# The first weight load of a two-branch decode kernel, cut after 16 partitions

## The chip, the cores and the metric

The kernel runs on one core of a Trainium2 chip. The metric is the time of one execution on the device in microseconds; the median of three runs of the kernel before is 825.76 us (825.72 to 825.88).

## What is computed

Two attention layers, A and B, each decode one token and their outputs are joined. Both have 32 heads of 128, a key and a value cache of 16384 positions, and bf16 data.

```
q   = x @ wq                                   # x: 512, wq: 512 x 4096
p   = softmax(q . k * 128**-0.5)               # per head
o   = p @ v
out = o @ wo                                   # wo: 4096 x 512
A: all 16384 positions;  B: the last 4096 positions alone
result = concat(A's out, B's out)              # 1024 numbers
```

Nearly all of the work is to read the caches: 134 MB of keys and as much of values for A, a quarter of that for B, and 4 MiB for each of the four weight matrices.

## The kernel before

The order of the work is written out by hand (`manual_schedule`), so each engine and each queue runs its instructions in the order of the program. The work goes through 20 steps `T`. A step of A takes two heads, a step of B eight; B's are steps 0, 7, 13 and 19. A step loads an 8 MiB tile of keys (for B in two halves of four heads) and later an equal tile of values. Keys stand in a ring of two buffers (`kring`), values in one buffer (`vring`).

For each half of a key tile VectorE multiplies the keys by q (line 227) and adds up along the head dimension in a tree (lines 233 and 237). TensorE and ScalarE do the softmax of the step before and its product with the values (`pv`, line 331), and fold the result into columns. At the end `project_out_rows` and `project_out_columns` multiply by A's and B's wo; B's wo is loaded in five pieces of falling size, last of all.

All large loads are issued by SyncE (SP), in program order, on one queue which 16 DMA engines serve together. ScalarE (ACT) issues six small loads at the start: x of B and x of A, each in three pieces (line 419). They are written into one partition of the tile `scratch`. The start goes so:

1. ACT issues x of B, then x of A.
2. SP issues wq of B into the first half of a value buffer (`wqt`), the first half of B's first keys, wq of A into the other half of `wqt`, and the second half of the keys.
3. VectorE writes constants and masks, and spreads x into the operands of the projections. `turn_x` (line 176) brings x from one row to 128 partitions by TensorE, for B and then for A.
4. `project_q` (line 203) multiplies by wq, for B and then for A. ScalarE copies the result (line 207), and VectorE's first product follows.

wq is laid out with four of its 512 rows in a partition: partition p holds rows 4p to 4p+3, 32 KiB in one run, in memory as in the buffer. `load_wq` copies all 128 partitions in one transfer.

The framework gives each transfer one of eight completion semaphores, in turn over all queues. A transfer therefore waits until the one eight places earlier has landed. Counted from the first x piece, the second half of B's first keys is eight places behind wq of B, and waits for it on SP.

Of the kernel before, what the change touches and what calls it, by code (L numbers as in the profile page):

```python
# [11 lines left out]
P = 128  # L12
# [5 lines left out]
CH = 128  # L18
# [7 lines left out]
def kernel(  # L26
# [14 lines left out]
    nc = tc.nc  # L41
# [5 lines left out]
    KC = D // P  # L47
# [13 lines left out]
    def kslot(name):  # L61
        return kring.tile([P, 2 * CH, DH], BF16, tag="kring", name=name)

    def vslot(name):
        return vring.tile([P, 2 * CH, DH], BF16, tag="vring", name=name)
# [8 lines left out]
    A, B = _Side(), _Side()  # L74
# [36 lines left out]
    def new_k(T):  # L111
        K[T] = kslot("kt")

    def load_k(T, u=None):
        s, g = steps[T]
        if s is A:
            nc.sync.dma_start(
                out=K[T][:, :, :].rearrange("p l d -> p (l d)"),
                in_=a_pair(A_k_cache, g).rearrange("p l d -> p (l d)"),
            )  # L120
        else:
            for v in (0, 1) if u is None else (u,):
                nc.sync.dma_start(
                    out=K[T][:, v * CH : (v + 1) * CH, :].rearrange("p l d -> p (l d)"),
                    in_=b_window(B_k_cache, 2 * g + v),
                )

    def load_v(T):
        s, g = steps[T]
        V[T] = vslot("vt")  # L130
        if s is A:
            nc.sync.dma_start(
                out=V[T][:, :, :].rearrange("p l d -> p (l d)"),
                in_=a_pair(A_v_cache, g).rearrange("p l d -> p (l d)"),
            )
        else:
            for u in (0, 1):
                load_v_half(T, u, V[T][:, u * CH : (u + 1) * CH, :])

    def load_v_half(T, u, dst):  # L140
        nc.sync.dma_start(  # L141
            out=dst.rearrange("p l d -> p (l d)"), in_=b_window(B_v_cache, 2 * steps[T][1] + u)
        )

    def load_wq(s, W):
        s.wq_t = W
        nc.sync.dma_start(
            out=W.rearrange("p a b -> p (a b)").rearrange("p (c f) -> p c f", c=KC),
            in_=s.wq.rearrange("(p c) f -> p c f", c=KC),
        )  # L150

    def load_wo(s, W, pieces):
        s.wo_t = W.rearrange("p a b -> p (a b)").rearrange("p (r f) -> p r f", r=HQ)
        src = s.wo.rearrange("(p r) f -> p r f", r=HQ)
        r = 0
        for n in pieces:
            nc.sync.dma_start(out=s.wo_t[:, r : r + n, :], in_=src[:, r : r + n, :])  # L157
            r += n

    def make_masks(s):  # L160
        nc.vector.tensor_reduce(out=s.mask[:, :], in_=by_head(s, identf[:, :]), axis=AX.X, op=ALU.add)
        n = 8 * s.groups // s.nh
        nc.vector.tensor_copy(
            s.rows[:, :, :, :], s.mask[:, :].unsqueeze(1).unsqueeze(3).broadcast_to([P, n, s.nh, 4])
        )
        for v in range(s.parts):
            w = 32 * s.groups
            block = identf[:, v * w : (v + 1) * w].rearrange("p (g r) -> p r g", g=s.groups)
            nc.vector.tensor_reduce(
                out=s.sel[:, v, :], in_=block[:, 0 : 4 * s.nh, :], axis=AX.X, op=ALU.add  # L170
            )
# [10 lines left out]
    def spread_x(s, flat):  # L182
        s.xb = flat[:, 0 : s.nh * KC * P].rearrange("p (h c m) -> p h c m", h=s.nh, c=KC)
        nc.vector.memset(s.xb, 0.0)
        turn_x(s)
        for j in range(s.nh):
            dst = s.xb[:, j, :, :]
            if s is A:
                dst = dst.rearrange("p c (h i) -> p c h i", h=s.nh)[:, :, j, :]
            else:  # L190
                dst = dst.rearrange("p c (i h) -> p c i h", h=s.nh)[:, :, :, j]
            nc.vector.tensor_copy(dst, s.xT[:, :].unsqueeze(2).broadcast_to([P, KC, P // s.nh]))

    def project_q(s):
        wq = s.wq_t.rearrange("p a b -> p (a b)").rearrange(
            "p (c g h d) -> p c h g d", c=KC, h=s.nh, d=DH
        )
        for g in range(0, HQ // s.nh, 4):
            qp = ps_t.tile([P, 4, DH], F32, tag="tp", name="qp")
            n = KC * s.nh  # L200
            for k in range(n):
                c, j = divmod(k, s.nh)
                nc.tensor.matmul(  # L203
                    qp[:, :, :], lhsT=s.xb[:, j, c, :], rhs=wq[:, c, j, g : g + 4, :],
                    start=(k == 0), stop=(k == n - 1),
                )
            nc.scalar.copy(s.q[:, g : g + 4, :], qp[:, :, :])  # L207
# [15 lines left out]
    def scores_prod(T, u):  # L223
        s, g = steps[T]
        k = K[T][:, u * CH : (u + 1) * CH, :]
        j = g if s is A else 2 * g + u
        nc.vector.tensor_tensor(out=k, in0=k, in1=s.q[:, j : j + 1, :].broadcast_to([P, CH, DH]), op=ALU.mult)  # L227
# [71 lines left out]
    def spread_p(un, a=0, b=2 * CH, write=on_scalar):  # L299
        p = un.p[:, a:b].rearrange("p (i c) -> p i c", c=4)  # L300
        for j in range(un.s.nh):
            write(un.pm[:, a // 4 : b // 4, j, :], p, un.s.mask[:, j : j + 1])
# [17 lines left out]
    def recip(un):  # L320
        un.r = small.tile([P, 8], F32, tag="r", name="r")
        n = un.s.parts * un.s.nh if un.last else 1
        nc.vector.reciprocal(un.r[:, 0:n], un.sm[:, 264 : 264 + n])
# [89 lines left out]
    with tc.manual_schedule():  # L413
        scratch = kslot("scratch")
        x0 = 4 * KC * P
        for s in (B, A):
            s.x_row = scratch[0:1, :, :].rearrange("p a b -> p (a b)")[:, x0 : x0 + D]
            for a, b in ((0, D // 4), (D // 4, D // 2), (D // 2, D)):
                nc.scalar.dma_start(out=s.x_row[:, a:b], in_=s.x[0, 0:1, a:b])  # L419
            x0 += D  # L420
        new_k(0)
        wqt = vslot("wqt")
        load_wq(B, wqt[:, 0:CH, :])
        load_k(0, 0)
        load_wq(A, wqt[:, CH : 2 * CH, :])
        load_k(0, 1)
        make_identity(nc, identf[:, :])
        nc.vector.memset(one_f[:, :], 1.0)
        nc.vector.memset(one_b[:, :], 1.0)
        nc.vector.memset(ones_col[:, :], 1.0)  # L430
        nc.vector.memset(A.o[:, :], 0.0)
        nc.vector.memset(B.o[:, :], 0.0)
        nc.vector.tensor_copy(ident[:, :], identf[:, :])
        spread_x(B, scratch[:, :, :].rearrange("p a b -> p (a b)"))
        for s in (B, A):
            make_masks(s)
        nc.vector.memset(pick[:, :], 0.0)
        nc.vector.tensor_copy(
            pick[:, 4 : 4 + P].rearrange("h (m k) -> h m k", k=4)[:, :, 0], identf[0:HQ, 0:HQ]
        )  # L440
        spread_x(A, one.tile([P, 2 * KC * P], BF16, tag="o4", name="xbA")[:, :])
        project_q(B)
        project_q(A)
        new_k(1)
        load_k(1)
        for T in range(NT):
            if T >= 1:
                load_v(T - 1)
                if T + 1 < NT:
                    new_k(T + 1)  # L450
                    load_k(T + 1)
            if T == NT - 1:
                W = kslot("wot")
                load_wo(A, W[:, 0:CH, :], (HQ,))
                load_v_half(T, 0, W[:, CH : 2 * CH, :])
            scores_prod(T, 0)
            if T >= 1:
                un = units[T - 1]
                max_all(un)
                soft(un)  # L460
                spread_p(un)
                soft_sum(un)
                pv(un)
            scores_tree(T, 0)
            if T >= 1:
                recip(un)
                evict(un)
                columns(un)
            scores_prod(T, 1)
            scores_tree(T, 1)  # L470
            if T < NT - 1:
                unit_max(units[T])
        Z = vslot("wot")
        load_v_half(NT - 1, 1, Z[:, 0:CH, :])
        load_wo(B, Z[:, CH : 2 * CH, :], wo_pieces)
        un = units[NT - 1]
        permute_o(A)
        project_out_rows(A)
        unit_max(un)
        max_all(un)  # L480
        soft(un)
        spread_p(un, 0, CH)
        spread_p(un, CH, 2 * CH, nc.vector.tensor_scalar_mul)
        soft_sum(un)
        recip(un)
        pv_columns(un, 0, W[:, CH : 2 * CH, :])
        pv_columns(un, 1, Z[:, 0:CH, :])
        permute_o(B)
        project_out_columns(B, wo_pieces)
# [30 lines left out]
```

## Time and profile before

| | before |
|---|---|
| median of 3 runs | 825.76 us |
| span of the profiled execution | 823.9 us |
| DVE (VectorE) busy | 763.9 us, 93% |
| PE (TensorE) busy | 202.7 us, 25% |
| ACT (ScalarE) busy | 60.1 us, 7% |
| load queue of SP (q1), time of its packets | 99.2% of 16 engines |
| read from HBM | 352.32 MB, 428 GB/s over the span |
| wq of B, from issue to landing | 12.3 us |
| VectorE's first product starts | 23.89 us |
| last load lands | 820.19 us |

The profile is one execution; its own time is known as the span, from the first to the last instruction, and the median of the runs is 1.9 us above it. Times within the profile count from the span's start. "SPq" and "ACTq" are the instructions with which these engines issue DMAs, "PEld" is TensorE's loading of weights. A row of waits names the instruction that waited, what released it, the microseconds in total, how often, and the longest. The chain that ended last is followed back from the last instruction to whatever released each step; its rows give start, length and what ran or was waited for.

### The profile page before, as it was taken

To read this page: it belongs to the slowest core of one execution; us is meant where nothing else is said; L and a number is where in the kernel's file an instruction comes from. 1 tells how busy PE (TensorE), PEld (TensorE's weight loads), DVE (VectorE), ACT (ScalarE), POOL (GpSimd) and SP (SyncE) were. 2 spreads that over 40 slices of the span, in tenths; PEclk is the share of its full clock that TensorE was granted. 3 is DMA by queue.
4 is the path that set the end of the run, shared out by engine and by line. 5 is a ranking of instruction groups with operands and counts; after the bars stand their busy time and mean duration, and the time that the engine had idled before them with its cause. 6 is when DMAs were issued, how large, how long until landed. Compare 5 with 4: busy or idle time off the path is not lost.

```text
span 823.9 us, 4724 instructions
## 1 busy us (share of the span) xinstructions
PE 202.7 (25%) x1985; PEld 100.7 (12%) x1985; DVE 763.9 (93%) x353; ACT 60.1 (7%) x168; POOL 0.7 (0%) x6
## 2 busy tenths in 40 slices
PE   2702212203030303130312213030303020303175
PEld 0201100101010101010101101010101010101035
DVE  2899999999999999999999999999999999999980
ACT  0101000001010000100000000010100000000010
POOL 0000000000000000000000000000000000000000
PEclk9865656565565555565555565565656565556585
DMA  9999999999999999999999999999999999999997
GB/s 384 434 433 433 453 420 443 430 436 440 423 446 420 424 439 443 412 453 420 443 417 449 414 452 410 450 417 428 438 449 424 436 433 430 443 414 445 418 429 296
DMA packets 8107, 352.62 MB, mean 428 GB/s; under 512 B 915, under 2 KB 1046, under 8 KB 1302
## 3 DMA queue, kind: packets, MB, share of 16 engines
q1 hardware_dynamic: 8072, 352.33, 99.2%
q8 instruction: 15, 0.25, 0.1%
q14 instruction: 6, 0.05, 0.0%
q10 hardware_dynamic: 14, 0.00, 0.0%
HBM read 352.32 MB, written 0.00 MB: 428 GB/s over the span
## 4 chain that ended last, share of the span: by engine, by line
DMA 82%; PE 15%; DVE 1%; SPq 0%; issue 0%; ACTq 0%; ACT 0%; DVEq 0%
DMA vt<-in_A_v_cache_dram 65%; DMA vt<-in_B_v_cache_dram 13%; PE oA L331 11%; DMA wot<-in_B_wo_dram 4%; PE oB L331 2%; PE qp L203 2%; DMA scratch<-in_A_x_dram 2%; DVE kt L227 1%; SPq L141 0%; ACTq L419 0%; SPq L157 0%; PE out_cols L397 0%; ACT qB L207 0%; PE out_rows L407 0%; DVE rows L409 0%
## 5 line engine op out<-in xcount | busy, mean ns | idle before, releaser
L233 DVE TENSOR_TENSOR kt<-kt 128x8192 bf16<-128x8192 bf16 (+3 forms) x160 | 344.9, 2156 | 4.8
L227 DVE TENSOR_TENSOR kt<-kt,qA 128x16384 bf16<-128x16384 bf16 x32 | 277.8, 8683 | 11.0 <-DMA kt<-in_A_k_cache_dram 10.9
L331 PE MATMUL oA<-vt,pm 128*8 128x512 bf16 x1024 | 92.3, 538 | 132.1 <-DMA vt<-in_A_v_cache_dram 132.1
L227 DVE TENSOR_TENSOR kt<-kt,qB 128x16384 bf16<-128x16384 bf16 x8 | 69.4, 8680 | 6.3 <-ACT qB L207 6.3
L249 PE MATMUL sm<-identf,m 128*1 128x128 f32 x24 | 8.1, 370 | 227.3 <-DVE m L244 227.3
L331 PEld LDWEIGHTS <-pm 128*8 128x8 bf16 (+1 forms) x1216 | 37.3, 111 | 216.7 <-issue 196.3
L268 PE MATMUL sm<-one_f,Mr 1*128 1x1 f32 x48 | 12.9, 347 | 176.7 <-DVE Mr L264 147.1
L237 DVE TENSOR_REDUCE sc<-kt 128x128 f32<-128x1024 bf16 x40 | 48.8, 1220 | 2.7
L276 ACT ACTIVATE bias<-sm 128x1 f32<-128x1 f32 (+1 forms) x20 | 3.4, 172 | 420.8 <-PE sm L268 420.8
L268 PEld LDWEIGHTS sm<-one_f,Mr 1*128 1x128 f32 x48 | 11.2, 298 | 183.6 <-DVE Mr L264 152.2
L249 PEld LDWEIGHTS sm<-identf,m 128*1 128x1 f32 x24 | 1.7, 79 | 229.3 <-issue 216.2
L340 ACT ACTIVATE o<-oA,r 128x512 f32<-128x512 f32 x16 | 11.0, 688 | 220.5 <-PE oA L331 220.5
L331 PE MATMUL oB<-vt,pm 128*16 128x512 bf16 x192 | 17.2, 494 | 20.3 <-DMA vt<-in_B_v_cache_dram 16.2
L348 PE MATMUL oc<-selA,o 128*128 128x2 f32 x128 | 16.9, 254 | 12.7 <-ACT o L340 12.7
L348 PEld LDWEIGHTS oc<-selA,o 128*128 128x128 f32 x128 | 15.5, 191 | 20.8 <-ACT o L340 20.8
L297 ACT ACTIVATE pm<-p,maskA 128x256 bf16<-128x256 bf16 x32 | 14.5, 500 | 0.5
L315 PE MATMUL sm<-cs,rowsA 128*128 128x1 f32 x32 | 9.4, 362 | 14.3 <-ACT p L282 14.3
L282 ACT ACTIVATE p<-sc,bias 128x256 bf16<-128x256 f32 (+1 forms) x24 | 11.3, 470 | 0.6
L203 PE MATMUL qp<-wqt,xbA 128*128 128x512 bf16 x32 | 8.8, 444 | 6.0 <-DVE kt L227 6.0
L315 PEld LDWEIGHTS sm<-cs,rowsA 128*128 128x128 f32 x32 | 8.0, 310 | 15.7 <-ACT p L282 15.7
L203 PE MATMUL qp<-wqt,scratch 128*128 128x512 bf16 x32 | 9.9, 486 | 0.0
L362 DVE TENSOR_TENSOR OB<-ocol,r 128x4 bf16<-128x4 f32 x2 | 0.3, 161 | 10.2 <-PE ocol L358 10.2
(71 smaller groups left out, 108.1 us busy)
## 6 DMA issues: line engine op xcount, KB each, us to landing
kt<-in_B_k_cache_dram SPq DMA_DIRECT2D x8, 4096.0 KB, 29.1
vt<-in_B_v_cache_dram SPq DMA_DIRECT2D x6, 4096.0 KB, 23.3
wot<-in_B_v_cache_dram SPq DMA_DIRECT2D x2, 4096.0 KB, 22.6
wqt<-in_B_wq_dram SPq DMA_DIRECT2D x1, 4096.0 KB, 12.3
wqt<-in_A_wq_dram SPq DMA_DIRECT2D x1, 4096.0 KB
wot<-in_A_wo_dram SPq DMA_DIRECT2D x1, 4096.0 KB
wot<-in_B_wo_dram SPq DMA_DIRECT2D x1, 2048.0 KB
wot<-in_B_wo_dram SPq DMA_DIRECT2D x1, 1024.0 KB
```

The source lines that it names most:

```text
L203: nc.tensor.matmul(qp[:, :, :], lhsT=s.xb[:, j, c, :], rhs=wq[:, c, j, g : g + 4, :], start=(k == 0), stop=(k == n - 1),)
L227: nc.vector.tensor_tensor(out=k, in0=k, in1=s.q[:, j : j + 1, :].broadcast_to([P, CH, DH]), op=ALU.mult)
L233: nc.vector.tensor_tensor(out=k[:, :, 0:w], in0=k[:, :, 0:w], in1=k[:, :, w : 2 * w], op=ALU.add)
L237: nc.vector.tensor_reduce(out=units[T].sc[:, u * CH : (u + 1) * CH], in_=k[:, :, 0:8], axis=AX.X, op=ALU.add)
L249: nc.tensor.transpose(un.sm[0:1, v * P : (v + 1) * P], m[:, v : v + 1], identf[:, :])
L268: nc.tensor.matmul(un.sm[:, 256 + v : 257 + v], lhsT=Mr[:, v * P : (v + 1) * P], rhs=one_f[:, :], start=True, stop=True,)
L282: nc.scalar.activation(out=un.p[:, v * n : (v + 1) * n], in_=un.sc[:, v * n : (v + 1) * n], func=ACT.Exp, scale=inv, bias=bias[:, v : v + ...
L297: nc.scalar.activation(out=out, in_=in_, func=ACT.Copy, scale=mask)
L315: nc.tensor.matmul(un.sm[v * w : (v + 1) * w, 264:265], lhsT=s.rows[:, :, :, :].rearrange("p r a b -> p (r a b)"), rhs=un.cs[:, v : v + 1] ...
L331: nc.tensor.matmul(s.o[r0 : r0 + un.rows, :], lhsT=un.pm[:, l, :, :].rearrange("p a b -> p (a b)"), rhs=V[un.T][:, 4 * l : 4 * l + 4, :], ...
L340: nc.scalar.activation(out=un.osb[:, :], in_=un.s.o[:, :], func=ACT.Copy, scale=un.r[:, 0:1])
L348: nc.tensor.matmul(oc[:, 0:w], lhsT=un.osb[:, j * P : (j + 1) * P], rhs=sel[:, j, :], start=(j == 0), stop=(j == 3),)
```

## The change

wq of B, the first large load, becomes two transfers on the same queue, one behind the other: partitions 0 to 15 (512 KiB), then partitions 16 to 127 (3.5 MiB). wq of A is still one transfer, and the order of all other work is as it was. SP has one DMA more; the completion semaphores of the transfers behind it move on by one place.

```diff
-    def load_wq(s, W):
+    def load_wq(s, W, cuts=(0, P)):
         s.wq_t = W
-        nc.sync.dma_start(
-            out=W.rearrange("p a b -> p (a b)").rearrange("p (c f) -> p c f", c=KC),
-            in_=s.wq.rearrange("(p c) f -> p c f", c=KC),
-        )
+        dst = W.rearrange("p a b -> p (a b)").rearrange("p (c f) -> p c f", c=KC)
+        src = s.wq.rearrange("(p c) f -> p c f", c=KC)
+        for a, b in zip(cuts, cuts[1:]):
+            nc.sync.dma_start(out=dst[a:b], in_=src[a:b])
...
-        load_wq(B, wqt[:, 0:CH, :])
+        load_wq(B, wqt[:, 0:CH, :], (0, 16, P))
         load_k(0, 0)
         load_wq(A, wqt[:, CH : 2 * CH, :])
         load_k(0, 1)
```

## The prediction

> **What bounds the kernel now.** I read the page's slices and queues first, then the windows at the start, SyncE's waits, the chain's two ends, and VectorE's waits.
>
> ```profile
> DVE   2899999999999999999999999999999999999980
> ...
> DMA   9999999999999999999999999999999999999997
> GB/s 384 434 433 433 453 420 443 430 436 440 423 446 420 424 439 443 412 453 420 443 417 449 414 452 410 450 417 428 438 449 424 436 433 430 443 414 445 418 429 296
> ...
> q1 hardware_dynamic: 8072, 352.33, 99.2%
> HBM read 352.32 MB, written 0.00 MB: 428 GB/s over the span
> ```
>
> The load queue is busy in every slice but the last, at one rate. 352.3 MB at the steady 432 GB/s would take 815.6 us of the 823.9 us span; the other 8 us are the lead-in, the tail and small gaps. So the kernel is one unbroken stream of loads, and every microsecond in which the 16 DMA engines move fewer bytes than usual is paid in full at the end.
>
> The windows of the start (columns: stretch, length, busy PE, PEld, DVE, ACT, POOL, clock, DMA share, GB/s):
>
> ```profile
> 0.00:2.00 2.00, 0.00 (x0) 0.00 (x0) 1.05 (x6) 0.00 (x0) 0.70 (x6) 1.00 0.53 148
> 2.00:4.00 2.00, 0.00 (x0) 0.00 (x0) 1.09 (x3) 1.18 (x1) 0.00 (x0) 1.00 0.88 344
> 24.00:40.00 16.00, 10.05 (x40) 4.01 (x39) 15.90 (x4) 2.00 (x4) 0.00 (x0) 0.79 1.00 432
> ```
>
> By 4.0 us the stream has moved 0.30 + 0.69 = 0.98 MB, which is 2.3 us at 432 GB/s: it behaves as if it began at 1.7 us. The 432 GB/s over 16 engines are 27.0 GB/s each, so one 32 KiB row of wq (4 rows of the matrix, one partition) takes one engine 1.21 us, and a 4 MiB load, eight rows per engine, 9.7 us.
>
> The chain, first its head, then its end, and three waits:
>
> ```profile
> 2.51 13.95 DMA scratch<-in_A_x_dram
> 16.46 0.14 issue
> 16.59 0.26 PE xps L176 x4
> 16.85 6.40 PE qp L203 x16
> 23.27 0.59 ACT qB L207
> 23.89 8.70 DVE kt L227
> ...
> 790.04 30.16 DMA wot<-in_B_wo_dram
> 820.19 0.04 issue
> 820.24 0.60 PE out_cols L397 x16
> ```
>
> ```profile
> SPq L123 <- DMA wqt<-in_B_wq_dram: 10.5, 1, 10.5
> ...
> DVE kt L227 <- DMA kt<-in_A_k_cache_dram: 10.9, 15, 1.4
> ...
> PE ocol L358 <- DMA wot<-in_B_v_cache_dram: 2.7, 1, 2.7
> ```
>
> VectorE's start at 23.89 hangs on A's x, which trickles in at 16.46 beside the large rows. But that start is not what sets the end: in 15 steps VectorE waits for K, 10.9 us in all, and at the end the values (2.7 us) and the last piece of wo (landed 820.19) are waited for. A VectorE that starts earlier only waits longer; one that starts late against the stream has up to 10.9 us to catch up.
>
> **The change, part by part.**
>
> *One more issue on SyncE.* wq of B was issued at 0.73 for 0.41 us. Now a 16-row issue comes first and the 112-row one behind it: one more issue of 0.33 to 0.63 us (the range of SyncE's load issues). The first K load slips from 1.19 to about 1.7. Cover: 4 MiB are queued ahead of it, 9.7 us. Cost 0. If the first rows are on their way sooner, at most the lag from issue to stream (1.72 - 0.73 = 1.0 us) can be gained; if the second piece comes up to one issue late, up to 0.6 us is lost. I take -0.3, since fewer rows have to be set up before all 16 engines have one.
>
> *Waits that move.* Completion semaphores are handed out in turn from eight, so a transfer waits for the one eight earlier (that is the 10.5 us wait above). With one more transfer the first K load waits for B's first x piece, wq of A for the new 16-row piece, the second K load for B's second x piece. Behind them on SyncE stand the other loads. Before, the fourth load was issued at 13.10, with the stream fed until about 22 (two loads of 9.7 us from 2 us on). Wq of A would have to be later than that to leave a hole; 16 rows land long before. The later loads have the same wait eight earlier as now. Cost 0; bound 0 to 1, if the 16 rows took the longest time below (19.4 us) and A's wq just missed.
>
> *Sixteen more completion writes*, one per engine: the page counts 915 packets under 512 B among 8107, nearly all of them such writes, in a queue whose time the data fills. Cost 0.
>
> *The first 16 rows.* In every transfer of the stream shown, 128 rows are in flight together, and 432 GB/s is seen only there. No row shows 16 engines writing into 16 neighbouring partitions. Bounds: if each row has its own way into SBUF, 16 rows take what one row per engine takes, 1.21 us: cost 0. If all 16 share one way of the rate that one engine shows, 16 x 1.21 = 19.4 us: cost 18.2. If SBUF is cut into 16 ways of eight neighbours each, the 16 rows have two, 8 x 1.21 = 9.7: cost 8.5. Between 0 and 8.5 I take four rows to a way, 4 x 1.21 = 4.85: cost 3.6, because the nearest rows, the eight rows that each engine writes in 9.7 us, say that engine and way are matched one to one over the whole width, and an eighth of the width cannot reach all the ways. The 3.6 falls on all 16 engines, and no later work gives it back.
>
> [...]
>
> *The other 112 rows.* Split over 16 engines that is seven rows each, where the ways fit blocks of eight or four. So engine blocks no longer line up with the ways, and two engines meet on one way part of the time while others stand free. Bounds: 0 (no sharing), and every one of seven rows doubled, 7 x 1.21 = 8.5. I take two rows of the seven doubled, the two that stick out of a block, 2.4. Of both terms some 0.3 lies beside the slow start that is there anyway (the lead-in of 1.72).
>
> *Who is late next.* wq of B lands some 5 us later and A's x, alternating with slowed rows on its engine, 4 to 10 later. So VectorE's first product goes from 23.9 to 28 to 34. Against a stream that is itself 5.4 late that is at most 4.6, under the 10.9 us that it has; the next K load of A, issued at 26.72 when B's projection is done, may come 14 us later before the queue (fed until 41) runs dry. Cost 0.
>
> Sum: -0.3 + 3.6 + 2.4 - 0.3 = +5.4 us. Span 823.9 + 5.4 = 829.3. The median of the runs, 825.76, is 1.9 above the profiled span; that margin stays, so 831.2.
>
> **The rivals.**
>
> *Rows are independent (not slower).* The stream finds full speed with any 16 rows; then only the first term is left, -0.3, and 825.5, between 824.8 (-1.0) and 826.4 (+0.6). For it: 27 GB/s could be the engines' own limit, and no row tells engine from way. Against it: the rate is the same to a per cent whatever the shape of the load, as a limit behind the engines would make it. Point of decision: whether the first 16 rows take more than about 2.5 us. 17%.
>
> *A wide way.* Ways carry twice an engine's rate: four rows take 2.4, cost 1.2, and at most as much again in the second piece, and the -0.3: 826.7 to 827.9, I say 827.3. Nothing for or against. 9%.
>
> *The 112 rows run like the 16.* If each engine takes every sixteenth row, all engines sit on the same few ways throughout: eight rows x 3.64 = 29 us, 854.9. For it: nothing says how seven rows are picked. Against: engines are at full rate with eight. 4%.
>
> *The change helps by A's x.* Between the pieces the x transfers could slip in early and VectorE start up to 3 us sooner (16.46 against wq's landing at 13.0). It gains nothing, because the stream has no hole to fill; it joins the first rival at 825.5.
>
> **How the numbers follow.** Shared ways 70%, 828.8 (the 3.6 without the 2.4) to 833.6 (four of the seven rows doubled, 4.8), point 831.2; all seven doubled, 837.3, is its far end; independent 17%; wide way 9%; the last 4%. A measurement of this kernel tells about 0.2%, 1.65 us: the lines are 824.1 and 827.4. Faster needs more than 1.65 out of a lead-in of 1.0 that can be gained, so 3%; same is the rest of the independent rival and part of the wide way, 18%; slower 79%. Range 825.4 to 834.5: it takes in most of the independent case below and leaves out the 4% and the upper tail. Within the likeliest case alone, 829 to 834.
>
> **What would show it.** In the windows, 2 to 6 us should move some 110 to 150 GB/s where 344 to 410 stand now, and from there to about 18 us less than 432. From 24 us on the rate must be 432 again. A first K load landing 5 us later, VectorE's first product at 28 or later, VectorE waiting for K about as much as before, and the last piece of wo landing at about 825.6 bear out the steps. I am wrong if the first window at 432 GB/s starts before 5 us: then the ways are not shared. If the loss shows but the end does not move, the stream had slack that I don't see; if the rate later than 24 us differs, something other than the first load was changed.

## The result: 9.4 us slower

The changed kernel takes 835.15 us (median of 4 runs, 835.11 to 835.21) against 825.75 us before, a ratio of 1.0114 (95% interval 1.01 to 1.0129). The forecast was slower by 5.4 us, 831.2, with a range up to 834.5: the direction and the place were right, the size was not, and the time lies just outside the range. The profiled span grew from 823.9 to 833.4 us.

The first fence has the slices and the load queue of the changed kernel's page.

```profile
DVE  2499999999999999999999999999999999999980
...
DMA  9999999999999999999999999999999999999996
GB/s 220 414 461 412 445 415 447 440 418 443 413 447 441 411 448 419 429 455 421 435 425 434 444 428 418 441 428 431 441 434 432 425 441 437 432 415 440 428 429 286
...
q1 hardware_dynamic: 8088, 352.33, 99.1%
```

The DMA engines show as busy as before, 9 in every slice but the last. Only the bytes tell: 220 GB/s in the first slice, where it was 384, and from the second on the same level as before. Here a busy DMA engine is not one that moves data at its rate. The 16 packets more (8088 after 8072, all 16 of them under 512 B: 931 after 915) are read as the completion writes of the one transfer more; the bytes are the same.

The windows of the start, with the columns as before (the last two are the DMA engines' busy share and GB/s); first four of the kernel before, then the changed kernel:

```profile
4.00:8.00 4.00, 0.00 (x0) 0.00 (x0) 0.00 (x0) 0.10 (x1) 0.00 (x0) 1.00 0.95 410
8.00:12.00 4.00, 0.26 (x4) 0.20 (x4) 1.20 (x8) 0.00 (x0) 0.00 (x0) 1.00 0.93 402
12.00:16.00 4.00, 0.00 (x0) 0.00 (x0) 1.54 (x9) 0.00 (x0) 0.00 (x0) 1.00 1.12 484
16.00:20.00 4.00, 3.41 (x12) 1.39 (x13) 0.66 (x3) 0.00 (x0) 0.00 (x0) 1.00 0.99 426
```

```profile
0.00:2.00 2.00, 0.00 (x0) 0.00 (x0) 1.05 (x6) 0.00 (x0) 0.70 (x6) 1.00 1.33 197
2.00:4.00 2.00, 0.00 (x0) 0.00 (x0) 1.09 (x3) 1.26 (x1) 0.00 (x0) 1.00 0.47 66
4.00:8.00 4.00, 0.00 (x0) 0.00 (x0) 0.00 (x0) 0.02 (x1) 0.00 (x0) 1.00 0.72 131
8.00:12.00 4.00, 0.00 (x0) 0.00 (x0) 0.00 (x0) 0.00 (x0) 0.00 (x0) 1.00 1.03 262
12.00:16.00 4.00, 0.26 (x4) 0.20 (x4) 2.59 (x15) 0.00 (x0) 0.00 (x0) 1.00 1.14 303
16.00:20.00 4.00, 0.00 (x0) 0.00 (x0) 0.15 (x1) 0.00 (x0) 0.00 (x0) 1.00 0.93 221
20.00:24.00 4.00, 1.08 (x7) 0.55 (x8) 0.66 (x3) 0.00 (x0) 0.00 (x0) 1.00 1.03 377
24.00:28.00 4.00, 4.00 (x12) 1.46 (x11) 0.00 (x0) 0.00 (x0) 0.00 (x0) 1.00 0.93 401
28.00:40.00 12.00, 4.28 (x20) 1.76 (x18) 7.59 (x1) 1.17 (x2) 0.00 (x0) 0.90 1.01 434
```

The loss stands wholly in the first 22 us. A window counts a packet, its bytes and its time, wholly where it starts; that is why a DMA share can pass 1.00. So twelve of the first 16 rows stand in 0 to 2 us (197 GB/s) and four in 2 to 4 us (66 GB/s); the 131 GB/s behind them are already the first 16 of the 112 rows. From 8 to 20 us, 262, 303 and 221 GB/s stand where 402, 484 and 426 stood, about 60%: these are the 112 rows, and their stretch is the longer one. The trace's own DMA records say it more closely. Each line below takes the next 16 packets of 32 KiB in order of their start. That this is one per engine is a reading; the records do not name the engine:

```
16 packets   before: start, duration (us)     after: start, duration (us)
1            1.76..2.88   1.21..2.03          1.76..2.09    3.28..3.81    <- 16 rows
2            3.48..4.25   1.21..1.23          5.08..5.85    2.65..3.23    <- 112 rows from here
3            4.70..5.46   1.21                8.16..8.49    2.26..2.38
4            5.91..6.67   1.21                10.43..10.75  1.67..2.28
5            7.12..7.88   1.21                12.26..13.02  1.77..2.06
6            8.33..9.09   1.21                14.03..14.85  1.86..2.40
7            9.54..10.30  1.21                15.88..17.07  2.26..2.36
8            10.75..11.51 1.21                18.14..19.34  2.04..2.29
9            11.96..12.72 1.21                20.30..21.50  1.55..1.91    <- first keys of B
10           13.17..13.93 1.21                22.20..23.24  1.22
```

Two things are to be seen. All packets of lines 1 to 9 are slow, none stays at 1.21 us. And at line 10 the stream is 9.0 to 9.3 us behind (22.20 - 13.17, 23.24 - 13.93), which is the loss of the whole kernel: nothing of it comes back in the 810 us that follow. By the same records the last packet of data ends at 829.48 us, 9.4 later than before (820.05), and the span ends 4.0 us behind it (before 3.8).

On the compute side the chain's head is pushed back, as the timeline of VectorE and the waits of the changed kernel show:

```profile
32.41 8.69 DVE L227 TENSOR_TENSOR kt<-kt,qB 128x16384 bf16<-128x16384 bf16 x1 [8.50 <-DMA kt<-in_B_k_cache_dram]
```

```profile
DVE kt L227 <- DMA kt<-in_A_k_cache_dram: 11.2, 16, 1.2
...
PE xps L176 <- DMA scratch<-in_A_x_dram: 9.7, 1, 9.7
...
DVE kt L227 <- DMA kt<-in_B_k_cache_dram: 9.1, 2, 8.5
```

VectorE's first product starts at 32.41 in place of 23.89, and it now waits for the first keys themselves. From there on it waits for A's keys as it did before (11.2 us in place of 10.9): it follows the stream.

### The profile page after: what moved, and what is told of

It is laid out like the page before. It is cut to its first block, busy times and chain, and to the rows that moved or that the text cites. A ratio compares the mean times of both kernels' runs of the same rounds, so it can differ in the third digit from the quotient of the medians.

```text
span 833.4 us, 4724 instructions
## 1 busy us (share of the span) xinstructions
PE 206.8 (25%) x1985; PEld 102.2 (12%) x1985; DVE 764.0 (92%) x353; ACT 60.1 (7%) x168; POOL 0.7 (0%) x6
## 3 DMA queue, kind: packets, MB, share of 16 engines
q1 hardware_dynamic: 8088, 352.33, 99.1%
## 4 chain that ended last, share of the span: by engine, by line
DMA 83%; PE 15%; issue 2%; SPq 0%; ACT 0%; DVE 0%; DVEq 0%
DMA vt<-in_A_v_cache_dram 63%; DMA vt<-in_B_v_cache_dram 12%; PE oA L331 11%; DMA wqt<-in_A_wq_dram 4%; PE oB L331 2%; DMA wot<-in_B_v_cache_dram 2%; PE qp L203 1%; DMA wqt<-in_B_wq_dram 1%; PE out_cols L397 0%; SPq L141 0%; PE out_rows L407 0%; ACT pm L297 0%; DVE rows L409 0%; PE op L374 0%; ACT oTs L371 0%
## 5 line engine op out<-in xcount | busy, mean ns | idle before, releaser
L227 DVE TENSOR_TENSOR kt<-kt,qA 128x16384 bf16<-128x16384 bf16 x32 | 277.8, 8682 | 11.2 <-DMA kt<-in_A_k_cache_dram 11.2
L268 PEld LDWEIGHTS sm<-one_f,Mr 1*128 1x128 f32 x48 | 11.2, 299 | 183.8 <-DVE Mr L264 152.3
L331 PE MATMUL oB<-vt,pm 128*16 128x512 bf16 x192 | 20.5, 578 | 20.4 <-DMA vt<-in_B_v_cache_dram 16.3
L383 PE MATMUL out_row<-wot,OpA 128*1 128x512 bf16 x32 | 9.6, 471 | 0.8 <-DMA wot<-in_A_wo_dram 0.8
```

What stands on the lines that cost most here:

```text
L268: nc.tensor.matmul(un.sm[:, 256 + v : 257 + v], lhsT=Mr[:, v * P : (v + 1) * P], rhs=one_f[:, :], start=True, stop=True,)
L331: nc.tensor.matmul(s.o[r0 : r0 + un.rows, :], lhsT=un.pm[:, l, :, :].rearrange("p a b -> p (a b)"), rhs=V[un.T][:, 4 * l : 4 * l + 4, :], ...
```

## The experiments

Theory S says that neighbouring partitions share a way into SBUF. A way is an assumed path by which DMA data reaches a group of partitions; the traces do not name it, and the groups are part of the theory. Its rivals: T, the extra transfer with its issue, completion writes and moved waits; R, something that holds only at the start of the stream. Within S it was open whether only the engines that share a way are slowed, as the prediction had it, or all 16.

### The same two sizes, cut along the columns

```diff
-        load_wq(B, wqt[:, 0:CH, :], (0, 16, P))
+        # shortened; for B alone: all 128 partitions, 4 KiB of each, then the other 28 KiB
+        for a, b in ((0, 2048), (2048, 16384)):
+            nc.sync.dma_start(out=dst[:, a:b], in_=src[:, a:b])
```

> wq of B in two transfers of 512 KiB and 3.5 MiB as in the change, but cut along the columns, so that both have all 128 partitions. Theory S, shared ways (neighbouring partitions share one of 16 ways into SBUF, each of about one engine's rate): nothing is shared, 825.5 within 0.5 us. Theory T, the extra transfer (issue, completion writes, the waits that move by one place): about +9.4, 835.2, as in the change. Theory R, cold start (two transfers at the very beginning disturb the start of the stream): also about +9.4.

Measured: 825.71 us (10 runs), ratio 1.0 (0.9991 to 1.0009). Its windows from 2 to 22 us (before, the same windows have 393 and 456 GB/s):

```profile
2.00:12.00 10.00, 0.26 (x4) 0.21 (x4) 3.83 (x18) 1.28 (x1) 0.00 (x0) 1.00 1.01 415
12.00:22.00 10.00, 8.96 (x34) 3.76 (x35) 0.66 (x3) 0.59 (x1) 0.00 (x0) 1.00 1.02 439
```

The same number of transfers, of the same sizes, with waits that move by the same one place, on full width (4 and 28 KiB of each partition): the stream keeps its rate and the time does not move. T falls. R falls as far as it rests on two transfers at the start.

### The same cut in the middle of the queue

```diff
-        load_wq(B, wqt[:, 0:CH, :], (0, 16, P))
+        load_wq(B, wqt[:, 0:CH, :])
...
-        load_wq(A, wqt[:, CH : 2 * CH, :])
+        load_wq(A, wqt[:, CH : 2 * CH, :], (0, 16, P))
```

> wq of B whole; wq of A, third in the queue and long after the start, is cut after 16 partitions. S: the same loss as in the change wherever the cut stands, +9 to +10.5 (the slow first rows of the start now don't hide a part), 835 to 836.3. R: 0 to +1. T: +9.4 only if the waits that move are the cause; these move by one place here as well.

Measured: 836.07 us, 10.3 us over before (825.75), ratio 1.0128 (1.0113 to 1.0144). The windows of this kernel, behind one of the kernel before, and its first product on VectorE:

```profile
22.00:27.00 5.00, 4.69 (x21) 1.85 (x19) 3.11 (x1) 0.86 (x2) 0.00 (x0) 1.00 1.00 433
```

```profile
12.00:22.00 10.00, 5.34 (x18) 2.14 (x19) 2.27 (x12) 0.00 (x0) 0.00 (x0) 1.00 1.10 439
22.00:27.00 5.00, 4.09 (x19) 1.67 (x17) 3.15 (x1) 1.17 (x2) 0.00 (x0) 1.00 1.11 170
27.00:42.00 15.00, 0.00 (x0) 0.00 (x0) 14.83 (x6) 0.00 (x0) 0.00 (x0) 0.65 0.94 245
```

```profile
23.85 8.69 DVE L227 TENSOR_TENSOR kt<-kt,qB 128x16384 bf16<-128x16384 bf16 x1 [6.20 <-DMA kt<-in_B_k_cache_dram]
```

The stream runs at 439 GB/s until the cut load's turn comes, then at 170 and 245. VectorE starts when it did before (23.85), and the end is still 10.3 us later. So the cut costs about as much third in the queue as first, R falls, and VectorE's late start in the changed kernel is a companion of the loss, not its cause. At the start about 0.9 us of the cost (10.3 less 9.4) is hidden. The intervals of the two ratios overlap; in the DMA records this stream is 10.0 to 10.2 us behind the one before, the changed kernel's 9.0 to 9.4. That the 0.9 hides beside the first packets, which are slow in the kernel before too (1.76 us on average in place of 1.21), is the likely reading, not a thing that was tested.

### Half and half, and the large piece first

```diff
-        load_wq(B, wqt[:, 0:CH, :], (0, 16, P))
+        load_wq(B, wqt[:, 0:CH, :], (0, 64, P))       # one kernel
+        load_wq(B, wqt[:, 0:CH, :], (0, 112, P))      # or, in another
```

> Cut after 64 partitions in place of 16. S: each half reaches only half of the ways, two engines on each, so eight rows take 2.43 us in place of 1.21: +9.7, 835.5. T: +9.4, the same as in the change, so this run alone does not tell the two apart. If rows were independent in SBUF: 0. R: +9.4 or less.

> The pieces the other way round: partitions 0 to 111, then 112 to 127. S with all engines held to the slowest of a round (the second piece costs as much whether it is first or second): +8 to +12, about 835. S where only the engines that share a way are slow: +4.1 to +6.6, 830 to 832.4. T: +9.4.

Measured: 836.37 us for halves (ratio 1.0129, 1.0113 to 1.0144), 835.21 us for 112 first (1.0115, 1.0098 to 1.0132). In the DMA records of the halves the packets take 2.53 to 2.59 us from the second line of 16 on (2.36 to 2.41 in the fifth, the first of the second half): somewhat more than twice 1.21, as theory S has it where only half of the ways are reached; the window from 12 to 22 us has 206 GB/s, where 456 stood before. If each engine took every sixteenth row, and a way took four rows as in the prediction's choice, four engines would meet on a way, 4.85 us by the same count; that is not there. Which rows an engine takes the records do not say. With 112 rows first, the loss (9.5 us) lies far over what slow sharers alone would give (4.1 to 6.6) and in the range given for all engines held up together.

### One unused load, 16 partitions or all

The next kernels are the kernel before with one load more, third in the queue, whose data nobody uses; each has one of the three last lines.

```diff
         load_k(0, 0)
+        spare = scratch[:, :, :].rearrange("p a b -> p (a b)")[:, 16384:32768]
+        more = A.wq.rearrange("(p c) f -> p (c f)", c=KC)
+        nc.sync.dma_start(out=spare[:, 0:2048], in_=more[:, 0:2048])    # control
+        nc.sync.dma_start(out=spare[0:16], in_=more[0:16])              # or 16 neighbours
+        nc.sync.dma_start(out=spare[0:128:8], in_=more[0:16])           # or 16 spread
         load_wq(A, wqt[:, CH : 2 * CH, :])
```

> The kernel before plus one load of 512 KiB that nobody uses, third in the queue, of 128 partitions by 4 KiB, into a free part of the tile scratch. Control: 512 KiB at 432 GB/s are 1.2 us, so about +1.2 to +1.5, 827.1, under every theory.

> The same 512 KiB at the same place, as partitions 0 to 15 by 32 KiB, which leaves all other transfers whole. S with four ways: four rows on each way, +4.8 to +5.2 (of which 1.2 are the bytes), 830.6 to 831. If the rate of the change's first rows (3.6 us) were all: +3.6, 829.4. Two ways: +9.7. Theory T: as the control, +1.2.

> The same 512 KiB as 16 partitions by 32 KiB, but every eighth partition (0, 8, ... 120) in place of neighbours. [...] If only the number of partitions counts and not where they lie: the same as with 16 neighbours, +4.8.

Measured against 825.84: control 827.11 (+1.3, ratio 1.0016, 1.0007 to 1.0025), 16 neighbours 831.19 (+5.4, 1.0062, 1.0047 to 1.0077), 16 spread 828.67 (+2.8, 1.0033, 1.0021 to 1.0046). The bytes alone are the 1.3 us; 16 neighbours cost 4.1 us on top, 16 spread partitions 1.6 (their runs, 828.19 to 829.01, lie clear of the control's, 826.93 to 827.50). The loads of 16 rows have the same bytes, the same number of partitions, 32 KiB in each, and read the same rows of wq from HBM: where the partitions lie in SBUF decides. In the DMA records the line with the unused rows takes 3.12 to 4.67 us with neighbours and 1.83 to 2.40 us with spread ones. The latter is up to twice 1.21, as if two rows met on a way; so partitions that are no neighbours would share a way too, but which ones is not shown. The neighbours are the prediction's first term by itself, 4.1 for 3.6.

The spread loads have a side effect. VectorE's clearing of `scratch` waits 23.6 us for the load, probably because the framework takes the strided piece for an overlap, and VectorE's first product starts at 33.27. The next run shows that this costs the end nothing that can be seen.

### Four partitions on four engines

```diff
+        ...                                                    # spare and more as above
+        nc.sync.dma_start(out=spare[0:4], in_=more[0:4])       # neighbours
+        nc.sync.dma_start(out=spare[0:16:4], in_=more[0:4])    # or partitions 0, 4, 8, 12
```

> An unused load of four partitions (0 to 3) by 32 KiB, third in the queue; only four of the 16 engines have a row of it. S with coupling (all engines slow while some share a way): the row of that moment takes clearly more than 1.21 us on all 16 engines. S without coupling: about 4.8 us on four engines and 1.21 on the other twelve. The end: +1.2 to +5, since it is set by the slowest engine in both cases.

> As the unused load of partitions 0 to 3 by 32 KiB, but of partitions 0, 4, 8 and 12, one on each of four ways. S with coupling: no way is shared, so nothing stalls; four engines have one row more, +0 to +1.3, 825.8 to 827.1, against the +4.4 seen with four neighbours. If four partitions on four engines are slow in themselves, +4.4 again.

Measured: the four neighbours 830.22 (one run; +4.4), the four spread 826.72 (+0.9, ratio 1.0012, 1.0002 to 1.0021). First a window and the queue of the kernel with four neighbours, then the same window with four spread:

```profile
22.00:27.00 5.00, 3.49 (x17) 1.37 (x14) 3.86 (x1) 1.17 (x2) 0.00 (x0) 1.00 0.94 184
...
q1 hardware_dynamic: 8080, 352.46, 99.0%
```

```profile
22.00:27.00 5.00, 1.34 (x4) 0.59 (x5) 2.57 (x13) 0.00 (x0) 0.00 (x0) 1.00 1.08 465
```

8080 packets are eight more than before: four rows and four completion writes, which is read as four engines that take part; the records do not name them. The other twelve go on with wq of A, a whole transfer, whose packets take 1.21 us in the kernel before. Were only the sharers slow, these twelve would still move 324 GB/s (27.0 each); the window shows 184. The DMA records:

```
16 packets in order of start (us)       four neighbours     four spread
the last of the first keys   (16)       1.21                1.21
the unused rows and wq of A  (17)       1.69..3.83          1.21
                             (18)       1.47..3.58          1.21
                             (19)       1.22..1.25          1.21
```

All 32 packets of lines 17 and 18 are slow, and only four of them are unused rows: the engines slow down in packets of a whole transfer too, which elsewhere shows no sharing (wq of A in the kernel before: 1.21 us). 128 KiB, 0.04% of the bytes, cost 0.5% of the time. The four spread rows, with the same bytes from the same place, cost 0.9; so the sharing by itself is about 3.5 us (4.4 less 0.9), and it falls on everything in flight. The coupling is shown; what couples the engines (a buffer or a path that they share) was not tested.

The spread load also settles the cover of a late VectorE, in its timeline and waits:

```profile
31.23 8.69 DVE L227 TENSOR_TENSOR kt<-kt,qB 128x16384 bf16<-128x16384 bf16 x1 [2.68 <-ACT qB L207]
```

```profile
DVE kt L227 <- DMA kt<-in_A_k_cache_dram: 5.2, 8, 1.2
```

VectorE starts 7.3 us later than before while the stream keeps its pace, and the end moves 0.9, less than the one row more (1.21 us) that four of the engines have to carry. VectorE's waits for A's keys fall from 10.9 us to 5.2: that is where the time is caught up.

### The second piece by itself, and 16-row pieces all the way

```diff
+        ...                                                             # spare and more as above
+        nc.sync.dma_start(out=spare[16:128], in_=more[16:128])          # unused, third in the queue
```

```diff
-        load_wq(A, wqt[:, CH : 2 * CH, :])
+        load_wq(A, wqt[:, CH : 2 * CH, :], tuple(range(0, P + 1, 16)))  # another kernel
```

> An unused load of partitions 16 to 127 by 32 KiB (3.5 MiB), third in the queue: the second piece of the change by itself. Its bytes are 8.5 us. S with the term of the prediction, two of seven rows doubled: +10.9. S with coupling, from the cut of wq of A (10.3) less the 16 neighbours (5.4 less 1.3 for their bytes): 8.5 + 6.2 = +14.7, 840.5. All seven rows doubled: +17.

> wq of A in eight pieces of 16 partitions each. S: each piece is four rows to a way; at the 5.3 us that 16 neighbours took, 8 x 5.3 - 9.7 = +33, 858.5; at an exact 4.85 us each +29, 855. T: eight transfers in place of one cost seven times what one more costs in the cut along the columns, 0.

Measured: the 112 rows 840.82 (+15.0 over 825.79; ratio 1.0183, 1.0166 to 1.02), eight pieces of 16 rows 851.76 (+26.0; 1.0315, 1.03 to 1.0331). The 112 rows carry 8.5 us of bytes, so their shape costs 6.5 us, not the 2.4 of the prediction. Seven lines of 16 packets take, on average, 1.81, 2.27, 1.79, 1.98, 2.09, 2.25 and 2.13 us: an average of 2.05 in place of 1.21, and no packet of them is at 1.21; the line behind them still takes 1.67. Added up, the eight lines lie 6.3 us above 1.21 each. The two parts, 4.1 and 6.5, make 10.6, close to the 10.3 of the cut in the middle of the queue.

For the eight pieces S had said +29 to +33, and +26.0 came: in the middle of the series 16 rows take 4.42 to 4.46 us, not 4.85 or 5.3. That is 16 rows in 4.43 us, 118 GB/s. It is the rate of the series, not shown to be that of four ways: the 16 packets of a line start over 2.0 us, so two pieces are under way at a time, and under theory S neighbouring pieces can lie on different ways. The 5.3 was too high since it was taken from a single piece, whose hold-up reaches into the rows behind it: with 16 neighbours the next line takes 2.52 us on average.

## Why the prediction was wrong in size

- **The bound, the stream of loads: right.** 9.0 to 9.3 us lost by 22 us appear as 9.4 at the end. No load issue or VectorE wait gave any of it back, and the rate came back as the prediction asked: 401 GB/s from 24 to 28 us, 434 from 28 to 40.
- **One more issue, moved waits, completion writes at 0: right.** The cut along the columns has all three and costs nothing. In it wq of A was issued at 4.45 us, long before the stream could run dry; in the changed kernel at 7.42, behind the 16 rows, as the prediction expected.
- **A gain of 0.3 from an earlier start, and 0.3 hidden in the lead-in: slightly under.** Together 0.6; the cut at the start is 0.9 cheaper than the same cut in the middle. All first 16 packets do start within 0.33 us in place of 1.12, but then take 3.28 us and more. The prediction's reading of the start was off: its 0.98 MB "by 4.0 us" counts packets that had only started. In the records the third 16 packets start at 4.70 to 5.46; two packets of 1.21 earlier the stream would have begun at 2.3 to 3.0 us, not at 1.7. So the lead-in in which a cost could hide, and out of which it gave "faster" its 3%, was larger than its 1.0 us.
- **The first 16 rows, 3.6: right in kind, 4.1 by themselves** (16 neighbours, less the bytes). The prediction had 128 rows in flight together; the records before show at most 18 packets of 32 KiB under way at a time. The two bounds were far apart and the choice of four rows to a way was the author's estimate, backed by an argument alone, so that it came this near is in part luck. That four neighbouring rows slow one another the runs show (+4.4 for partitions 0 to 3, +0.9 for 0, 4, 8 and 12); how many partitions a way takes they do not. In the series of pieces a row of 4.43 us costs 3.2 above 1.21; the single piece costs more, and its records show the line behind it held up too.
- **The other 112 rows, 2.4: the step that failed.** "I take two rows of the seven doubled", with others that "stand free" meanwhile, let each engine pay only for its own meetings. The runs show 6.5, and no packet of the 112 rows at 1.21 us. The four neighbours show why: while they are written, packets of the other engines are held up too (all 32 of two lines over 1.21 us, up to 3.83), so none stands free. The bound above, all seven doubled, 8.5, whose time lay outside the range given, was nearer than the one below. The measured 6.5 lies between; which row each engine takes in which order, and so why it is not 8.5, stays open.
- **VectorE late but covered: right.** A's x was in use at 22.9 us, 6.3 later (forecast 4 to 10), the first product at 32.41 (forecast 28 to 34), and the end is not theirs: the four spread partitions delay VectorE by 7.3 us and the end by 0.9.
- **The rivals.** Independent rows: refuted, 3.28 to 3.81 us for the first rows against the 2.5 given as the point of decision. A way of twice the rate: refuted, since two engines on a way would then keep 1.21 us a row, and the halves take 2.57. The 112 rows like the 16 (854.9): did not come, and the eight pieces show what it would have been near, 851.8.

With 4.1 and 6.5 in place of 3.6 and 2.4, and 0.9 in place of 0.6, the same sum gives +9.7 against the 9.4 measured. The 0.9 is itself taken from measured times, so only the two parts of the cost bear this sum out.

## What to carry to other kernels

Here a load was better cut along its free dimension than along its partitions: the same two sizes cost 0 one way and 9.4 us the other, and even halves cost 10.6. The loads of this kernel never pause, and a narrow transfer was paid for by everything in flight, not by its own bytes (128 KiB in four neighbouring partitions: +4.4 us). Look for it in GB/s by window (184 in that run), since the slices show the DMA engines as busy as ever (a 9 at 220 GB/s as at 384). And when a sum has a term with ends far apart, ask whether those who are not part of a jam can pass it before choosing the low end.

## What the runs showed that was not expected

- Four neighbouring partitions on four engines slow all that is in flight: 184 GB/s over 5 us, +4.4 us for 128 KiB; partitions 0, 4, 8 and 12 in their place +0.9.
- Sharing is not quite proportional. In a steady stretch a line of 16 rows takes 1.21 us on the full width, 2.57 on half of it (2.1 times), and 4.43 in a series of pieces of 16 partitions (3.7 times). Why the last is under the four times of four rows to a way is not shown; that neighbouring pieces overlap is the likely reading.
- The order of pieces hardly matters: 16 then 112 rows +9.4, 112 then 16 rows +9.5.
